# Row loads turned into columns on TensorE, and fifteen tiny loads behind the last weights, in a gated decode kernel

## The chip, the cores and the metric

One core of a Trainium2 chip runs the whole program. The time is device microseconds of one execution; the median of several runs is compared. One execution is also recorded by the hardware profiler, and all profile rows come from that one.

## What is computed

One token of width 512 goes through two branches that a gate mixes. Branch A is attention over a cache of 4096 positions with 32 heads of 128; branch B is a dense layer with squared ReLU. B_x is not used. The reference, cut down:

```python
x = A_x                                                  # [1, 1, 512], bf16
g = sigmoid((x * gate_w).sum(-1, keepdims=True))
q = (x @ wq).reshape(1, 1, 32, 128)                      # wq 512 x 4096
p = softmax(einsum("bhqd,bhkd->bhqk", q, k) * 128**-0.5) # k, v: 32 x 4096 x 128
a = einsum("bhqk,bhkd->bhqd", p, v) @ wo                 # wo 4096 x 512
h = relu(x @ w1 + b1); h = h * h                         # w1 512 x 1376
b = h @ w2 + b2                                          # w2 1376 x 512
out = g * a + (1 - g) * b
```

K and V are 32 MB each, wq and wo 4 MB each, w1 and w2 1.4 MB each. x, gate_w, b1 and b2 are 1 to 2.75 KB.

## The kernel before

**Queues.** SP issues nearly all loads, in an order written out by hand: the four slices of wq, seven heads of K, then for each head one load of V (`load_v`) and one of K seven heads ahead (`load_k`, LAG = 7), with w1 put behind head 8 and w2 behind head 10. A head's K or V is 1 MB, one load; 8 slots each. A K load waits until the head eight before it was used by DVE (s_sd) and by PE (s_t), a V load until the PV matmuls of the head eight before it are done (s_pv). The upper half of wo follows at the end: `wox` (L247), three chunks (L249) that each have a semaphore, and then the store of `out` (L252) when `fin4` is ready (s_f4). GpSimd (POOL) loads the lower half of wo into the place of wq once the last q rows are read. ACT issues only the five small loads at the start (L296 to L300): x, gate weights, b1 in two parts and b2. Three of the vectors are laid out as columns: `col` gives partition p the elements p·j of the flat vector, so that x is 128 pieces of 8 bytes, and the last 96 entries of b1 are 96 pieces of 2 bytes.

**Start.** DVE forms the gate's partial products (L536), PE sums them over partitions with a ones matrix (L345), ACT and DVE make the sigmoid `gcol` and `omg` = 1 − g. DVE spreads x over 128 columns (`xb`). PE makes q twice: as columns `qcol` (128 matmuls of 128x128 on one column of x, L351), copied out by DVE (L549), and as rows spread over all partitions (`q_rows`, L361, eight groups of four heads), copied to `qb` by ACT (L308).

**Heads.** For half of a head's positions, DVE multiplies K with the q rows and sums (`ttr`, L561, 16 per head). The other half is transposed on PE (`transposes`, L375), copied from PSUM by ACT (`evac`, L316) and multiplied with the q column on PE (`scores`, L385). DVE takes the copy of these scores and the maximum (`smax`). Every four heads PE and DVE find a common maximum (`max_rows`, `gmax`, `max_cols`) and ACT takes the exponentials. PV (`pv`, L412) runs LAG heads behind. One loop over i = 0 to 38 in each engine's program sets the order: head i is transposed and multiplied, head i − 1 scored, head i − 7 goes through PV.

**Branch B and the output.** At i = 24 PE multiplies w1 with the x columns (`mlp_h`, L428), DVE adds b1, takes ReLU and square (`mlp`), and PE multiplies w2 into the accumulator (`mlp_out`). The first 16 heads' outputs are turned and regrouped with a 0/1 selector `selA` (`turn_a`, `spread_a`, L452), then multiplied with the lower half of wo at i = 28 to 31 (`out_a`, L463). The other 16 heads go through `regroup` with the selector `selB` (built by GpSimd inside `w1_sb` once `mlp_h` has read it, L285), `out_b` (L488), the sum with the scaled b2 (L639), a transpose (L527), a copy (L641) and the store.

Of the kernel before, what the change touches and what calls it, by code (L numbers as in the profile page):

```python
# [5 lines left out]
def bass_gated_mix__gqa_block_cached__dense_activation_squared_relu__decode_kernel(  # L6
# [63 lines left out]
    with ctx:  # L70
# [18 lines left out]
        selB = w1_sb[0:NH - NA, 0, 0:1024].rearrange("h (c p) -> h c p", c=8)  # L89
        w2a = sb("w2a", [128, FG, DM], bf16)  # L90
# [3 lines left out]
        gwcol = sb("gwcol", [128, 4], bf16)  # L94
        b1a = sb("b1a", [128, FG], bf16)
        b1b = sb("b1b", [FR, 1], bf16)
        b2r = sb("b2r", [4, 128], bf16)
        selA = sb("selA", [NA, 4, 128], bf16)
# [12 lines left out]
        negs = sb("negs", [G, 128], fp32)  # L111
# [10 lines left out]
        gj = sb("gj", [128, 4], bf16)  # L122
        zp = sb("zp", [128, 1], fp32)
# [4 lines left out]
        hp = sb("hp", [128, FG + 1], fp32)  # L128
# [19 lines left out]
        Q = pX[:, 64:64 + NH]  # L148
# [32 lines left out]
        s_cst = sem("s_cst")  # L181
        s_xf = sem("s_xf")
# [30 lines left out]
        s_out = sem("s_out")  # L213

# [3 lines left out]
        @block.sync  # L218
        def _(eng):
            for t in range(4):  # L220
                eng.dma_start(wq_sb[:, t, :], wq_v[:, t, :]).then_inc(s_wq[t], 16)  # L221

            def load_k(h):
                if h >= NK:
                    eng.wait_ge(s_sd, h - NK + 1)
                    eng.wait_ge(s_t, 2 * (h - NK + 1))
                eng.dma_start(Kt[:, h % NK, :], k_h[h, :, :]).then_inc(s_k[h % NK], 16)  # L227

            def load_v(h):
                if h >= NV:  # L230
                    eng.wait_ge(s_pv, h - NV + 1)
                eng.dma_start(Vt[:, h % NV, :], v_h[h, :, :]).then_inc(s_v[h % NV], 16)  # L232

            for h in range(LAG):
                load_k(h)
            for h in range(NH):
                load_v(h)
                if h + LAG < NH:
                    load_k(h + LAG)
                if h == 8:  # L240
                    for t in range(4):
                        eng.dma_start(w1_sb[:, t, :], w1_v[:, t, :]).then_inc(s_w1, 16)
                if h == 10:
                    eng.dma_start(w2a[:, :, :], w2_v).then_inc(s_w2, 16)
                    eng.dma_start(w2b[:, :], B_w2[FG * 128:F, :]).then_inc(s_w2, 16)
            eng.wait_ge(s_wa, 1)
            eng.dma_start(wox, A_wo[HX * 128:HX * 128 + 128, :]).then_inc(s_wx, 16)  # L247
            for c in range(NW):
                eng.dma_start(wo_sb[:, TS[c]:TS[c + 1], :], wob_v[:, TS[c]:TS[c + 1], :])\  # L249
                   .then_inc(s_wo[c], 16)  # L250
            eng.wait_ge(s_f4, 1)
            eng.dma_start(out[0, 0, :].rearrange("(j p) -> j p", p=128), fin4[:, :]).then_inc(s_out, 16)  # L252
            eng.wait_ge(s_out, 16)

        @block.gpsimd
        def _(eng):
            eng.memset(ident[:, :], 0.0).then_inc(s_id, 1)
            eng.memset(identf[:, :], 0.0).then_inc(s_id, 1)
            eng.memset(onesf[:, :], 1.0).then_inc(s_cst, 1)  # L260
            eng.memset(negs[:, :], -SCALE).then_inc(s_cst, 1)
            eng.memset(selA[:, :, :], 0.0).then_inc(s_id, 1)
            eng.wait_ge(s_id, 3)
            for m in (ident, identf):
                eng.affine_select(out=m[:, :], in_=m[:, :], compare_op=ALU.not_equal, fill=1.0,
                                  base=0, pattern=[[-1, 128]], channel_multiplier=1)\
                   .then_inc(s_id, 1)
            eng.affine_select(out=selA[:, :, :], in_=selA[:, :, :], compare_op=ALU.not_equal, fill=1.0,
                              base=A0, pattern=[[1, 4], [-1, 128]], channel_multiplier=4)\
               .then_inc(s_id, 1)  # L270
            eng.wait_ge(s_qps, 8)
            HI = A0 + 4 * (HX + 1)
            LO = A0 + 4 * HX
            for r in range(4):
                eng.inc_swdge_sem([], [], mode="reset_dge_cursor")
                src = B_w1[0:4, 0:32].rearrange("p (a c) -> p a c", a=2)
                eng.dma_start(dm[0:4, r, :, 0:8], src[:, :, 0:8]).then_inc(s_dm[r], 16)  # L277
                eng.dma_start(W[HI + r:A0 + 64:4, :], woa_v[HI - A0 + r:64:4, :],
                              max_dma_last_dim=8192).then_inc(s_wp[2 * r], 16)
                eng.dma_start(W[A0 + r:LO:4, :], woa_v[r:LO - A0:4, :],  # L280
                              max_dma_last_dim=8192).then_inc(s_wp[2 * r + 1], 16)
            for q in s_dm:
                eng.wait_ge(q, 16)
            eng.wait_ge(s_h, 1)
            eng.memset(selB, 0.0).then_inc(s_sb, 1)  # L285
            eng.wait_ge(s_sb, 1)
            eng.affine_select(out=selB, in_=selB, compare_op=ALU.not_equal, fill=1.0,
                              base=0, pattern=[[1, 8], [-1, 128]], channel_multiplier=8)\
               .then_inc(s_sb, 1)
# [3 lines left out]
        def _(eng):  # L293
            def col(ap):
                return ap.rearrange("(p j) -> p j", p=128)
            eng.dma_start(xcol[:, :], col(A_x[0, 0, :])).then_inc(s_x, 16)  # L296
            eng.dma_start(gwcol[:, :], col(gate_w)).then_inc(s_x, 16)
            eng.dma_start(b1a[:, :], col(B_b1[0:FG * 128])).then_inc(s_b, 16)
            eng.dma_start(b1b[:, :], B_b1[FG * 128:F].rearrange("(p j) -> p j", j=1)).then_inc(s_b, 16)
            eng.dma_start(b2r[:, :], B_b2.rearrange("(j p) -> j p", p=128)).then_inc(s_b, 16)  # L300
            eng.wait_ge(s_x, 32)
            eng.activation(xcolf[:, :], xcol[:, :], ACT.Copy).then_inc(s_xf, 1)
# [39 lines left out]
        def _(eng):  # L342
            eng.wait_ge(s_cst, 2)
            eng.wait_ge(s_zp, 1)
            eng.matmul(Z, onesf[:, :], zp[:, :], start=True, stop=True).then_inc(s_z, 1)  # L345
            for t in range(4):
                eng.wait_ge(s_wq[t], 16)
            eng.wait_ge(s_ez, 1)
            for h in range(NH):
                for t in range(4):  # L350
                    mm = eng.matmul(Q[:, h:h + 1], wq_sb[:, t, h * 128:(h + 1) * 128],  # L351
                                    xcol[:, t:t + 1], start=(t == 0), stop=(t == 3))
            mm.then_inc(s_q, 1)
# [3 lines left out]
            def q_rows(c):  # L357
                if c >= 1:
                    eng.wait_ge(s_qb, c)
# [3 lines left out]
                mm.then_inc(s_qps, 1)  # L363

# [14 lines left out]
            def scores(h):  # L379
                if h >= 1:  # L380
                    eng.wait_ge(s_cp, h)
                for y in range(YB):
# [14 lines left out]
            def max_cols(g):  # L397
                eng.wait_ge(s_dg, g + 1)
                eng.matmul(MB[:, G * g:G * g + G], negs[:, :], dg[:, g, :],
                           start=True, stop=True).then_inc(s_mb, 1)  # L400

            def pv(h):
# [4 lines left out]
                if h == HPO:  # L407
                    eng.wait_ge(s_qc, 1)
                if h == 3 * HPO:
                    eng.wait_ge(s_qb, 8)  # L410
# [10 lines left out]
            def mlp_h():  # L421
                eng.wait_ge(s_w1, 64)
                eng.wait_ge(s_on, 2)
                for n in range(FG + 1):
                    M = 128 if n < FG else FR
                    for t in range(4):
                        lhs = w1_sb[:, t, n:FG * 128:FG] if n < FG else w1_sb[:, t, FG * 128:F]
                        mm = eng.matmul(H[0:M, n:n + 1], lhs, xcol[:, t:t + 1],  # L428
                                        start=(t == 0), stop=(t == 3))
# [19 lines left out]
            def spread_a():  # L449
                eng.wait_ge(s_ac, 1)  # L450
                for c in range(4):
# [17 lines left out]
            def regroup():  # L469
# [6 lines left out]
                eng.wait_ge(s_sb, 2)  # L476
# [18 lines left out]
            eng.wait_ge(s_id, 6)  # L495
            eng.wait_ge(s_b, 48)
            eng.transpose(KP[2][:, 0:4], b2r[:, :], ident[0:4, 0:4]).then_inc(s_b2, 1)
            eng.wait_ge(s_qc, 1)
            for i in range(NH + LAG):
# [4 lines left out]
                if i % 3 == 0 and i // 3 + 1 < 8:  # L504
                    q_rows(i // 3 + 1)
                if i >= 5 and (i - 5) % 4 == 0 and (i - 5) // 4 < NG:
# [24 lines left out]
        def _(eng):  # L531
# [4 lines left out]
            eng.tensor_tensor_reduce(gj[:, :], xcol[:, :], gwcol[:, :], 1.0, 0.0, ALU.mult,  # L536
# [11 lines left out]
            eng.wait_ge(s_q, 1)  # L548
            eng.tensor_copy(qcol[:, :], Q).then_inc(s_qc, 1)  # L549
# [22 lines left out]
            def gmax(g):  # L572
# [3 lines left out]
                eng.tensor_scalar(dg[:, g, :], identf[0:G, 0:G], gm[:, g:g + 1], None, ALU.mult)\  # L576
# [15 lines left out]
            def mlp():  # L592
                eng.wait_ge(s_h, 1)
                eng.tensor_tensor(hp[:, 0:FG], H[:, 0:FG], b1a[:, :], ALU.add).then_inc(s_hv, 1)
                eng.tensor_tensor(hp[0:FR, FG:FG + 1], H[0:FR, FG:FG + 1], b1b[:, :], ALU.add)\
                   .then_inc(s_hv, 1)
                eng.wait_ge(s_hv, 2)
                eng.tensor_scalar(hr[:, 0:FG], hp[:, 0:FG], 0.0, None, ALU.max).then_inc(s_hv, 1)
                eng.tensor_scalar(hr[0:FR, FG:FG + 1], hp[0:FR, FG:FG + 1], 0.0, None, ALU.max)\
                   .then_inc(s_hv, 1)  # L600
                eng.wait_ge(s_hv, 4)
# [7 lines left out]
            for i in range(NH + LAG):  # L609
                if i < NH:  # L610
                    ttr(i)
                if 1 <= i <= NH:
                    smax(i - 1)
                if i >= 5 and (i - 5) % 4 == 0 and (i - 5) // 4 < NG:
# [55 lines left out]
```

## Time and profile before

| | |
|---|---|
| median of 3 runs | 199.59 us (199.5 to 199.74) |
| the profiled execution | 199.66 us, its span 197.9 us |
| busy PE / PEld / DVE / ACT / POOL | 130.1 / 117.2 / 128.8 / 79.0 / 11.4 us |
| bytes moved, mean rate | 78.76 MB, 398 GB/s |
| DMA packets | 12560, of them 2336 under 512 B |
| K load, V load, from issue to landing (median) | 26.5 us, 27.3 us |
| wo chunks by SP, from issue to landing | 16.2, 17.6 and 17.8 us |
| the longest waits of PE and DVE | for K loads: 32.5 us (L375), 27.8 us (L561) |
| SP waits for fin before the store (L252) | 18.6 us |

The span runs from the first to the last recorded instruction; some 1.8 us of the execution lie outside it. PEld are weight loads, which overlap the matmuls (PE). "SPq" in the chain is the time that SP takes to issue a load, and a row "DMA" is the time from an issue to its landing, the stay in the queue included. Idle time of an engine that does not set the end costs nothing.

### The profile page before, as it was taken

The page shows a single profiled execution, that of the slowest core. Times are in us where ns is not written, and L with a number is a line of the kernel's source. Part 1 is how long each engine was busy: PE and PEld are TensorE (multiplying, and loading weights), DVE is VectorE, ACT ScalarE, POOL GpSimd, SP SyncE. Part 2 cuts the span into 40 slices and gives each one's busy share as a digit, 9 for nine tenths or more (in the row PEclk, how much of TensorE's full clock was granted, in tenths as well). Part 3 has the DMA queues.
Part 4 walks back from the last instruction along what each step waited for, and adds up shares of the span by engine and source line. Part 5 has one row for each costly group of instructions (what it writes and reads, how often), then busy time and mean ns, then how long its engine had stood idle before and what let it go on. Part 6 is the DMA issues. An engine that isn't in the chain of part 4 may idle for free.

```text
span 197.9 us, 6756 instructions
## 1 busy us (share of the span) xinstructions
PE 130.1 (66%) x2535; PEld 117.2 (59%) x2542; DVE 128.8 (65%) x1139; ACT 79.0 (40%) x147; POOL 11.4 (6%) x26
## 2 busy tenths in 40 slices
PE   0109946579897977716617476746978986995454
PEld 0107744459777767616615476746977886995443
DVE  0100899999999997707816778747799776760010
ACT  2000854737638536413307433533256331633000
POOL 4000000000000000000002910000210000000000
PEclk9999985855557555555557655555555555555555
DMA  6999999999999999999999999999999999999970
GB/s 194 413 375 427 421 421 419 424 417 421 421 414 416 421 417 411 419 418 397 406 422 412 419 416 411 413 422 416 424 411 422 419 416 419 421 419 419 411 307 33
DMA packets 12560, 78.76 MB, mean 398 GB/s; under 512 B 2336, under 2 KB 2560, under 8 KB 3328
## 3 DMA queue, kind: packets, MB, share of 16 engines
q1 hardware_dynamic: 11208, 76.36, 93.9%
q0 software_dynamic: 768, 1.97, 2.5%
q8 instruction: 20, 0.33, 0.7%
q10 hardware_dynamic: 552, 0.01, 0.2%
q14 instruction: 12, 0.10, 0.1%
HBM read 78.32 MB, written 0.00 MB: 396 GB/s over the span
## 4 chain that ended last, share of the span: by engine, by line
DMA 69%; DVE 14%; SPq 7%; PE 7%; issue 1%; ACT 0%; DVEq 0%
DMA Kt<-in_A_k_cache_dram 54%; DVE Kt L561 13%; DMA W<-in_A_wo_dram 9%; DMA W<-in_A_wq_dram 6%; SPq L232 5%; PE KP L375 2%; PE pX L351 2%; DVE S L561 1%; SPq L227 1%; PE pQ L361 1%; SPq L221 1%; PE pX L488 1%; PE pX L463 0%; PE pQ L412 0%; PE pX L412 0%
## 5 line engine op out<-in xcount | busy, mean ns | idle before, releaser
L561 DVE CUSTOM_DVE_ANT_0 Kt<-Kt,qb 128x128 bf16<-128x128 bf16 x512 | 112.1, 288 | 28.3 <-DMA Kt<-in_A_k_cache_dram 27.8
L316 ACT ACTIVATE kT<-KP 128x1024 bf16<-128x1024 bf16 x64 | 61.8, 1023 | 68.5 <-PE KP L375 68.5
L375 PE MATMUL KP<-ident,Kt 128*128 128x128 bf16 x512 | 55.6, 294 | 32.8 <-DMA Kt<-in_A_k_cache_dram 32.5
L375 PEld LDWEIGHTS KP<-ident,Kt 128*128 128x128 bf16 x512 | 48.2, 137 | 35.5 <-DMA Kt<-in_A_k_cache_dram 34.2
L561 DVE DVE_READ_ACCUMULATOR2_ANT S<- 128x1 f32 x512 | 41.6, 81 | 0.0
L385 PEld LDWEIGHTS pS<-qcol,kT 128*128 128x128 bf16 x512 | 18.6, 107 | 11.1 <-DVE S L567 10.8
L385 PE MATMUL pS<-qcol,kT 128*128 128x1 bf16 x512 | 19.1, 167 | 9.2 <-DVE S L567 8.9
L412 PEld LDWEIGHTS pO<-E,Vt 128*128 128x128 bf16 x512 | 15.5, 104 | 1.2 <-issue 0.8
L412 PE MATMUL pO<-E,Vt 128*128 128x1 bf16 x512 | 16.1, 165 | 0.0
L361 PE MATMUL pQ<-W,xb 128*128 128x512 bf16 x25 | 11.2, 581 | 1.7 <-issue 1.7
L412 PE MATMUL pQ<-E,Vt 128*128 128x1 bf16 x256 | 8.0, 165 | 6.3 <-DMA Vt<-in_A_v_cache_dram 6.3
L412 PEld LDWEIGHTS pQ<-E,Vt 128*128 128x128 bf16 x256 | 7.6, 104 | 6.7 <-issue 6.6
L308 ACT ACTIVATE qb<-pQ 128x512 bf16<-128x512 f32 x8 | 4.7, 592 | 16.4 <-PE pQ L361 16.4
L327 ACT ACTIVATE E<-S,nM 128x32 bf16<-128x32 f32 x32 | 9.9, 309 | 0.3
L277 POOL DMA_DIRECT2D dm<-in_B_w_dram x4 | 2.6, 648 | 104.4 <-PE pQ L361 104.4
L412 PEld LDWEIGHTS pX<-E,Vt 128*128 128x128 bf16 x256 | 7.8, 104 | 0.7 <-issue 0.6
L412 PE MATMUL pX<-E,Vt 128*128 128x1 bf16 x256 | 8.1, 165 | 0.0
L351 PE MATMUL pX<-xcol,W 128*128 128x1 bf16 x128 | 3.6, 165 | 4.9 <-DMA W<-in_A_wq_dram 4.9
L345 PE MATMUL pX<-zp,onesf 128*128 128x1 f32 x2 | 0.6, 347 | 9.3 <-DVE zp L536 9.3
L570 DVE TENSOR_REDUCE mp<-S 128x1 f32<-128x32 f32 x32 | 6.0, 186 | 1.1
L351 PEld LDWEIGHTS pX<-xcol,W 128*128 128x128 bf16 x128 | 3.5, 104 | 4.9 <-issue 4.9
L582 DVE RECIPROCAL rden<-pM 128x8 f32<-128x8 f32 x4 | 0.8, 200 | 8.1 <-PE pM L418 8.1
(83 smaller groups left out, 76.2 us busy)
## 6 DMA issues: line engine op xcount, KB each, us to landing
Kt<-in_A_k_cache_dram SPq DMA_DIRECT2D x32, 1024.0 KB, 26.5
Vt<-in_A_v_cache_dram SPq DMA_DIRECT2D x32, 1024.0 KB, 27.3
W<-in_A_wq_dram SPq DMA_DIRECT2D x4, 1024.0 KB, 8.4
W<-in_A_wo_dram POOLq DMA_DIRECT2D x4, 384.0 KB, 12.8
w_sb<-in_B_w_dram SPq DMA_DIRECT2D x4, 344.0 KB, 22.2
w2a<-in_B_w_dram SPq DMA_DIRECT2D x1, 1280.0 KB, 18.7
W<-in_A_wo_dram SPq DMA_DIRECT2D x1, 1024.0 KB, 16.2
W<-in_A_wo_dram SPq DMA_DIRECT2D x1, 768.0 KB, 17.6
```

The source lines that it names most:

```text
L232: eng.dma_start(Vt[:, h % NV, :], v_h[h, :, :]).then_inc(s_v[h % NV], 16)
L277: eng.dma_start(dm[0:4, r, :, 0:8], src[:, :, 0:8]).then_inc(s_dm[r], 16)
L308: eng.activation(qb[:, c * 512:(c + 1) * 512], pQ[:, :], ACT.Copy).then_inc(s_qb, 1)
L316: eng.activation(kT[:, h % 2, j * HB * 128:(j + 1) * HB * 128], KP[n % 3][:, :], ACT.Copy).then_inc(s_ev, 1)
L327: eng.activation(E[:, h % NE, :], S[:, h % NS, :], ACT.Exp, bias=nM[:, h:h + 1], scale=SCALE, accum_out=RS[:, h:h + 1]).then_inc(s_e, 1)
L351: mm = eng.matmul(Q[:, h:h + 1], wq_sb[:, t, h * 128:(h + 1) * 128], xcol[:, t:t + 1], start=(t == 0), stop=(t == 3))
L361: mm = eng.matmul(pQ[:, :], xb[:, t, :], wq_sb[:, t, c * 512:(c + 1) * 512], start=(t == 0), stop=(t == 3))
L375: mm = eng.transpose(KP[n % 3][:, y * 128:(y + 1) * 128], Kt[:, h % NK, b * 128:(b + 1) * 128], ident[:, :])
L385: mm = eng.matmul(S2[:, y:y + 1], kT[:, h % 2, y * 128:(y + 1) * 128], qcol[:, h:h + 1], start=True, stop=True)
L412: mm = eng.matmul(O(h, h + 1), Vt[:, h % NV, b * 128:(b + 1) * 128], E[:, h % NE, b:b + 1], start=(b == 0), stop=(b == NB - 1))
L561: ins = eng.tensor_tensor_reduce(kb, kb, qb[:, h * 128:(h + 1) * 128], 1.0, 0.0, ALU.mult, ALU.add, S[:, h % NS, b:b + 1])
L570: eng.tensor_reduce(mp[:, h:h + 1], S[:, h % NS, :], AX.X, ALU.max).then_inc(s_mp, 1)
```

## The change

- **Rows for columns.** x, gate_w and b1 are loaded as one row each, on one partition (x and the gate into a corner of `w1_sb`, which w1 overwrites later), b2 as before but into `w1_sb`. PE makes the x columns from the row with four matmuls against a 1x1 identity (XC); ACT copies them out twice (fp32, bf16). The gate's sum is one DVE reduction over the row. b1 enters `mlp_h` as one more matmul per group of outputs, and DVE's two adds go.
- **q columns from q rows.** The 128 matmuls of L351 go. `q_cols(c)` takes the four heads' columns out of `qb` with four matmuls against an identity column, and DVE copies them (`qcol_copy`), in eight groups: group 0 ahead of the loop, the others two rounds behind their q rows. `q_rows(c)` now waits for that copy (s_qc) in place of s_qb, `scores(h)` waits for its group's copy.
- **Memory and constants.** `selA` is built inside `w1_sb` at the place where `selB` is, ahead of it, and `spread_a` waits for it; the constant `negs` goes, its factor sits in DVE's `gmax`. SP waits for s_z and s_b2 ahead of the w1 loads.
- **Fifteen tiny loads.** Behind the last wo chunk SP issues loads of n rows of 16 bytes, n = 1 to 15, into a part of `w1_sb` that nothing reads, and waits for them after the store.

The diff, cut to its core:

```diff
+        selA = w1_sb[0:NA, 1, 0:512].rearrange("h (c p) -> h c p", c=4)
+        xrow = w1_sb[0:1, 0, 0:DM]
+        grow = w1_sb[0:1, 1, 0:DM]
+        b1r = sb("b1r", [1, F], bf16)
+        b2r = w1_sb[0:4, 2, 0:128]
+        XC = pO[:, 0:4]
+        Q = pQ[:, 0:4]
...
 @block.sync
                 if h == 8:
+                    eng.wait_ge(s_z, 1)
+                    eng.wait_ge(s_b2, 1)
...
+            for n in range(1, 16):
+                eng.dma_start(w1_sb[0:n, 3, 32 * n:32 * n + 8], B_w1[0:n, 0:8]).then_inc(s_pr[n - 1], 16)
             eng.wait_ge(s_f4, 1)
             eng.dma_start(out[0, 0, :].rearrange("(j p) -> j p", p=128), fin4[:, :]).then_inc(s_out, 16)
             eng.wait_ge(s_out, 16)
+            for q in s_pr:
+                eng.wait_ge(q, 16)
...
 @block.gpsimd
-            eng.memset(selB, 0.0).then_inc(s_sb, 1)
+            eng.memset(w1_sb[0:NA, 0:2, 0:1024], 0.0).then_inc(s_sb, 1)
             eng.wait_ge(s_sb, 1)
+            eng.affine_select(out=selA, in_=selA, compare_op=ALU.not_equal, fill=1.0,
+                              base=A0, pattern=[[1, 4], [-1, 128]], channel_multiplier=4)\
+               .then_inc(s_sb, 1)
...
 @block.scalar
-            eng.dma_start(xcol[:, :], col(A_x[0, 0, :])).then_inc(s_x, 16)
-            eng.dma_start(gwcol[:, :], col(gate_w)).then_inc(s_x, 16)
-            eng.dma_start(b1a[:, :], col(B_b1[0:FG * 128])).then_inc(s_b, 16)
-            eng.dma_start(b1b[:, :], B_b1[FG * 128:F].rearrange("(p j) -> p j", j=1)).then_inc(s_b, 16)
-            eng.dma_start(b2r[:, :], B_b2.rearrange("(j p) -> j p", p=128)).then_inc(s_b, 16)
-            eng.wait_ge(s_x, 32)
-            eng.activation(xcolf[:, :], xcol[:, :], ACT.Copy).then_inc(s_xf, 1)
+            eng.dma_start(xrow, A_x[0, :, :]).then_inc(s_x, 16)
+            eng.dma_start(grow, gate_w.rearrange("(a n) -> a n", a=1)).then_inc(s_x, 16)
+            eng.dma_start(b1r[:, :], B_b1.rearrange("(a n) -> a n", a=1)).then_inc(s_b, 16)
+            eng.dma_start(b2r, B_b2.rearrange("(j p) -> j p", p=128)).then_inc(s_b, 16)
+            eng.wait_ge(s_xc, 1)
+            eng.activation(xcolf[:, :], XC, ACT.Copy).then_inc(s_xf, 1)
+            eng.wait_ge(s_xf, 1)
+            eng.activation(xcol[:, :], xcolf[:, :], ACT.Copy).then_inc(s_xf, 1)
...
 @block.tensor
+            for t in range(4):
+                mm = eng.matmul(XC[:, t:t + 1], xrow[:, t:DM:4], ident[0:1, 0:1], start=True, stop=True)
+            mm.then_inc(s_xc, 1)
...
-            for h in range(NH):
-                for t in range(4):
-                    mm = eng.matmul(Q[:, h:h + 1], wq_sb[:, t, h * 128:(h + 1) * 128],
-                                    xcol[:, t:t + 1], start=(t == 0), stop=(t == 3))
-            mm.then_inc(s_q, 1)
...
+            def q_cols(c):
+                eng.wait_ge(s_qb, c + 1)
+                for n in range(4):
+                    h = 4 * c + n
+                    mm = eng.matmul(Q[:, n:n + 1], qb[:, h * 128:(h + 1) * 128], ident[:, 0:1],
+                                    start=True, stop=True)
+                mm.then_inc(s_q, 1)
...
+                    eng.matmul(H[0:M, n:n + 1], b1r[:, n:FG * 128:FG] if n < FG else b1r[:, FG * 128:F],
+                               ident[0:1, 0:1], start=True, stop=False)
...
+                if i % 3 == 2 and i // 3 + 1 < 8:
+                    q_cols(i // 3 + 1)
...
 @block.vector
-            eng.tensor_tensor_reduce(gj[:, :], xcol[:, :], gwcol[:, :], 1.0, 0.0, ALU.mult,
+            eng.tensor_tensor_reduce(grow, xrow, grow, 1.0, 0.0, ALU.mult,
...
-                eng.tensor_tensor(hp[:, 0:FG], H[:, 0:FG], b1a[:, :], ALU.add).then_inc(s_hv, 1)
-                eng.tensor_tensor(hp[0:FR, FG:FG + 1], H[0:FR, FG:FG + 1], b1b[:, :], ALU.add)\
```

More of the change, by code (lines that the diff above doesn't have):

```diff
@@ L93, in bass_gated_mix__gqa_block_cached__dense_activation_squared_relu__decode_kernel @@
         xcolf = sb("xcolf", [128, 4], fp32)
[L94 to L98, printed above, removed]
+        xrow = w1_sb[0:1, 0, 0:DM]
+        grow = w1_sb[0:1, 1, 0:DM]
+        b1r = sb("b1r", [1, F], bf16)
+        b2r = w1_sb[0:4, 2, 0:128]
         onA = sb("onA", [128, NA], bf16)
@@ L110, in bass_gated_mix__gqa_block_cached__dense_activation_squared_relu__decode_kernel @@
         onesf = sb("onesf", [128, 128], fp32)
-        negs = sb("negs", [G, 128], fp32)
         qcol = sb("qcol", [128, NH], bf16)
@@ L121, in bass_gated_mix__gqa_block_cached__dense_activation_squared_relu__decode_kernel @@
         onorm = sb("onorm", [128, NH], bf16)
-        gj = sb("gj", [128, 4], bf16)
-        zp = sb("zp", [128, 1], fp32)
+        zp = sb("zp", [1, 1], fp32)
         ez = sb("ez", [128, 1], fp32)
@@ L127, in bass_gated_mix__gqa_block_cached__dense_activation_squared_relu__decode_kernel @@
         omg = sb("omg", [128, 1], fp32)
-        hp = sb("hp", [128, FG + 1], fp32)
         hr = sb("hr", [128, FG + 1], fp32)
@@ L147, in bass_gated_mix__gqa_block_cached__dense_activation_squared_relu__decode_kernel @@
         Z = pX[:, 0:1]
-        Q = pX[:, 64:64 + NH]
+        XC = pO[:, 0:4]
+        Q = pQ[:, 0:4]
         H = pX[:, 128:128 + FG + 1]
@@ L181, in bass_gated_mix__gqa_block_cached__dense_activation_squared_relu__decode_kernel @@
         s_cst = sem("s_cst")
+        s_xc = sem("s_xc")
         s_xf = sem("s_xf")
@@ L213, in bass_gated_mix__gqa_block_cached__dense_activation_squared_relu__decode_kernel @@
         s_out = sem("s_out")
+        s_pr = [sem(f"s_pr{n}") for n in range(15)]
         block = ctx.enter_context(nc.Block())
@@ L260, in _ @@
             eng.memset(onesf[:, :], 1.0).then_inc(s_cst, 1)
-            eng.memset(negs[:, :], -SCALE).then_inc(s_cst, 1)
-            eng.memset(selA[:, :, :], 0.0).then_inc(s_id, 1)
-            eng.wait_ge(s_id, 3)
+            eng.wait_ge(s_id, 2)
             for m in (ident, identf):
@@ L267, in _ @@
                    .then_inc(s_id, 1)
-            eng.affine_select(out=selA[:, :, :], in_=selA[:, :, :], compare_op=ALU.not_equal, fill=1.0,
-                              base=A0, pattern=[[1, 4], [-1, 128]], channel_multiplier=4)\
-               .then_inc(s_id, 1)
             eng.wait_ge(s_qps, 8)
@@ L293, in _ @@
         def _(eng):
-            def col(ap):
-                return ap.rearrange("(p j) -> p j", p=128)
-            eng.dma_start(xcol[:, :], col(A_x[0, 0, :])).then_inc(s_x, 16)
-            eng.dma_start(gwcol[:, :], col(gate_w)).then_inc(s_x, 16)
-            eng.dma_start(b1a[:, :], col(B_b1[0:FG * 128])).then_inc(s_b, 16)
-            eng.dma_start(b1b[:, :], B_b1[FG * 128:F].rearrange("(p j) -> p j", j=1)).then_inc(s_b, 16)
-            eng.dma_start(b2r[:, :], B_b2.rearrange("(j p) -> j p", p=128)).then_inc(s_b, 16)
-            eng.wait_ge(s_x, 32)
-            eng.activation(xcolf[:, :], xcol[:, :], ACT.Copy).then_inc(s_xf, 1)
+            eng.dma_start(xrow, A_x[0, :, :]).then_inc(s_x, 16)
[6 more added lines that the diff above has]
+            eng.activation(xcol[:, :], xcolf[:, :], ACT.Copy).then_inc(s_xf, 1)
             eng.wait_ge(s_z, 1)
@@ L342, in _ @@
         def _(eng):
-            eng.wait_ge(s_cst, 2)
+            eng.wait_ge(s_cst, 1)
+            eng.wait_ge(s_id, 3)
+            eng.wait_ge(s_x, 32)
+            for t in range(4):
+                mm = eng.matmul(XC[:, t:t + 1], xrow[:, t:DM:4], ident[0:1, 0:1], start=True, stop=True)
+            mm.then_inc(s_xc, 1)
             eng.wait_ge(s_zp, 1)
-            eng.matmul(Z, onesf[:, :], zp[:, :], start=True, stop=True).then_inc(s_z, 1)
+            eng.matmul(Z, onesf[0:1, :], zp[:, :], start=True, stop=True).then_inc(s_z, 1)
             for t in range(4):
                 eng.wait_ge(s_wq[t], 16)
-            eng.wait_ge(s_ez, 1)
-            for h in range(NH):
-                for t in range(4):
-                    mm = eng.matmul(Q[:, h:h + 1], wq_sb[:, t, h * 128:(h + 1) * 128],
-                                    xcol[:, t:t + 1], start=(t == 0), stop=(t == 3))
-            mm.then_inc(s_q, 1)
             eng.wait_ge(s_xb, 4)
@@ L358, in q_rows @@
                 if c >= 1:
-                    eng.wait_ge(s_qb, c)
+                    eng.wait_ge(s_qc, c)
                 for t in range(4):
@@ L381, in scores @@
                     eng.wait_ge(s_cp, h)
+                eng.wait_ge(s_qc, h // 4 + 1)
                 for y in range(YB):
@@ L398, in max_cols @@
                 eng.wait_ge(s_dg, g + 1)
-                eng.matmul(MB[:, G * g:G * g + G], negs[:, :], dg[:, g, :],
+                eng.matmul(MB[:, G * g:G * g + G], onesf[0:G, :], dg[:, g, :],
                            start=True, stop=True).then_inc(s_mb, 1)
@@ L406, in pv @@
                     eng.wait_ge(s_on, h // HPO - 1)
-                if h == HPO:
-                    eng.wait_ge(s_qc, 1)
                 if h == 3 * HPO:
-                    eng.wait_ge(s_qb, 8)
+                    eng.wait_ge(s_qc, 8)
                 for b in range(NB):
@@ L428, in mlp_h @@
                         mm = eng.matmul(H[0:M, n:n + 1], lhs, xcol[:, t:t + 1],
-                                        start=(t == 0), stop=(t == 3))
+                                        start=False, stop=(t == 3))
                 mm.then_inc(s_h, 1)
@@ L450, in spread_a @@
                 eng.wait_ge(s_ac, 1)
+                eng.wait_ge(s_sb, 2)
                 for c in range(4):
@@ L475, in regroup @@
                                start=False, stop=False, skip_group_check=True)
-                eng.wait_ge(s_sb, 2)
+                eng.wait_ge(s_sb, 3)
                 eng.wait_ge(s_oc, 1)
@@ L494, in _ @@
             q_rows(0)
[L495 to L498, printed above, removed]
+            q_cols(0)
+            eng.wait_ge(s_id, 4)
+            eng.wait_ge(s_b, 32)
+            eng.transpose(KP[2][:, 0:4], b2r, ident[0:4, 0:4]).then_inc(s_b2, 1)
             for i in range(NH + LAG):
@@ L547, in _, with qcol_copy @@
             eng.tensor_scalar(omg[:, :], gcol[:, :], -1.0, 1.0, ALU.mult, ALU.add).then_inc(s_g, 1)
-            eng.wait_ge(s_q, 1)
-            eng.tensor_copy(qcol[:, :], Q).then_inc(s_qc, 1)
+            def qcol_copy(c):
+                eng.wait_ge(s_q, c + 1)
+                eng.tensor_copy(qcol[:, 4 * c:4 * c + 4], Q).then_inc(s_qc, 1)
+            qcol_copy(0)
             eng.wait_ge(s_g, 3)
@@ L575, in gmax @@
                 eng.wait_ge(s_gm, g + 1)
-                eng.tensor_scalar(dg[:, g, :], identf[0:G, 0:G], gm[:, g:g + 1], None, ALU.mult)\
+                eng.tensor_scalar(dg[:, g, :], identf[0:G, 0:G], gm[:, g:g + 1], -SCALE, ALU.mult, ALU.mult)\
                    .then_inc(s_dg, 1)
@@ L593, in mlp @@
                 eng.wait_ge(s_h, 1)
-                eng.tensor_tensor(hp[:, 0:FG], H[:, 0:FG], b1a[:, :], ALU.add).then_inc(s_hv, 1)
-                eng.tensor_tensor(hp[0:FR, FG:FG + 1], H[0:FR, FG:FG + 1], b1b[:, :], ALU.add)\
+                eng.tensor_scalar(hr[:, 0:FG], H[:, 0:FG], 0.0, None, ALU.max).then_inc(s_hv, 1)
+                eng.tensor_scalar(hr[0:FR, FG:FG + 1], H[0:FR, FG:FG + 1], 0.0, None, ALU.max)\
                    .then_inc(s_hv, 1)
                 eng.wait_ge(s_hv, 2)
[L598 to L601, printed above, removed]
                 eng.scalar_tensor_tensor(out=hs[:, 0:FG], in0=hr[:, 0:FG], scalar=omg[:, 0:1],
@@ L613, in _ @@
                     smax(i - 1)
+                if i % 3 == 2 and i // 3 + 1 < 8:
+                    qcol_copy(i // 3 + 1)
                 if i >= 5 and (i - 5) % 4 == 0 and (i - 5) // 4 < NG:
```

## The prediction

> **What bounds the kernel now.** I read the page first, then the chain of waits in order of time, the windows of the first and the last microseconds, the timeline of SP and the DMA packet records. Part 2 of the page, in 40 slices of 4.95 us:
>
> ```profile
> DMA  6999999999999999999999999999999999999970
> GB/s 194 413 375 427 421 421 419 424 417 421 421 414 416 421 417 411 419 418 397 406 422 412 419 416 411 413 422 416 424 411 422 419 416 419 421 419 419 411 307 33
> ```
>
> The 16 DMA engines are busy from the second slice to the 38th at about 420 GB/s, so 1 MB takes 2.5 us. No compute engine comes near that: PE is busy 66%, DVE 65%. Part 3 says whose bytes these are:
>
> ```profile
> q1 hardware_dynamic: 11208, 76.36, 93.9%
> q0 software_dynamic: 768, 1.97, 2.5%
> q8 instruction: 20, 0.33, 0.7%
> q10 hardware_dynamic: 552, 0.01, 0.2%
> q14 instruction: 12, 0.10, 0.1%
> ```
>
> q1 is SP's queue (all of K, V and the weights), q10 is ACT's, which carries only the five small loads that the change rewrites. The shares add to 97.4%; the rest is the 1.8 us before the first packet and the end. The end of the chain:
>
> ```profile
> 171.88 0.04 issue
> 171.93 1.89 PE KP L375 x16
> 173.81 0.41 PE pS L385 x16
> 174.22 0.85 PE pQ L412 x32
> 175.07 0.87 PE pX L463 x32
> ...
> 175.96 0.33 SPq L247
> 176.28 0.04 issue
> 176.33 0.43 SPq L249
> 176.76 0.04 issue
> 176.80 17.64 DMA W<-in_A_wo_dram
> 194.44 0.05 issue
> 194.48 1.02 PE pX L488 x32
> ```
>
> The wo chunk is issued at 176.80 and lands 17.64 us later: seven loads' worth of queue stands before it. K loads wait 26.5 us (median, part 6), eleven loads' worth. So whatever PE, DVE or ACT does some microseconds sooner or later changes only how long a load stands in the queue. The end is set by the time the queue needs, plus a fixed tail (last wo matmuls, fin, transpose, copy, out store) of 3.4 us. Windows of the last stretch (length, busy time of PE, PEld, DVE, ACT, POOL, clock, DMA share, GB/s):
>
> ```profile
> 190.00:191.00 1.00, 0.91 (x32) 0.82 (x31) 0.00 (x0) 0.00 (x0) 0.00 (x0) 0.50 0.65 270
> 192.00:193.00 1.00, 0.68 (x15) 0.49 (x16) 0.17 (x1) 0.00 (x0) 0.00 (x0) 0.50 0.52 209
> 194.00:195.00 1.00, 0.52 (x19) 0.52 (x20) 0.00 (x0) 0.00 (x0) 0.00 (x0) 0.50 0.09 33
> ```
>
> From 190 to 195 the DMA share falls step by step: some engines are done at 190, the slowest at 195. What counts is the work of the slowest engine.
>
> **The change, part by part.** All sums are made against the profiled execution: 199.66 us, a span of 197.9 and 1.76 outside it. The median of the runs is 199.59, 0.07 less.
>
> *Column loads become row loads.* Before, x, gate and b1 arrive in pieces of 8, 8, 20 and 2 bytes per partition: 128 + 128 + 128 + 96 pieces, with b2's 4 that is 484; four loads with 16 completion marks and one with 4 make 68 more, together the 552 packets of q10. After, three rows and b2: 52 pieces and 52 marks if a row is spread over 16 engines, 14 packets if not. At least 448 of 552 go. q10's 0.2% of 197.9 us is 0.40 us on every engine (0.30 to 0.49 by the rounding), and 448/552 of it is 0.32 us (0.24 to 0.40). If a row is not spread, one engine takes 4.8 KB more, which at 26 KB/us (420 GB/s over 16) is 0.18 us, still less than it sheds. I take 0.30, all of it on the path, as every engine carries some 34 of these packets between its big ones.
>
> *The hole in the stream.* These windows show the rate while and after q10 is at work:
>
> ```profile
> 11.00:12.00 1.00, 0.00 (x0) 0.00 (x0) 0.00 (x0) 0.00 (x0) 0.00 (x0) 1.00 1.04 410
> 12.00:13.00 1.00, 0.00 (x0) 0.00 (x0) 0.00 (x0) 0.00 (x0) 0.00 (x0) 1.00 0.82 262
> 13.00:14.00 1.00, 0.00 (x0) 0.00 (x0) 0.00 (x0) 0.00 (x0) 0.00 (x0) 1.00 0.91 370
> 14.00:15.00 1.00, 0.27 (x11) 0.30 (x12) 0.00 (x0) 0.00 (x0) 0.00 (x0) 1.00 1.01 426
> 15.00:16.00 1.00, 1.00 (x44) 1.00 (x41) 0.00 (x0) 0.00 (x0) 0.00 (x0) 1.00 1.03 434
> ```
>
> Against 430 GB/s the stretch from 11 to 14 loses (20 + 168 + 60)/430 = 0.58 us, with engines idle between packets although SP has loads waiting to be accepted. The packet records put the 96 two-byte pieces of b1b (with their marks) between 10.5 and 13.7 us, and the engines never idle like this again before 189. I lay the hole to these pieces, though the first of them pass at full rate, so it may be the turn from wq to K. Bounds 0 and 0.58; taken 0.45, since part of the 0.58 is already in the 0.30.
>
> The Trainium skill (DMA: Bandwidth & Descriptors, Specifications) says that below 512 B the engine does read-modify-write; 8-byte pieces pass here at 414 GB/s (6 to 8 us), so the trace shows no large price of that for them. The same page (Rules for kernel authors) says that a one-partition row fans out over 16 engines in few descriptors, and that it isn't measured which shape is faster.
>
> *q columns from q rows.* 128 matmuls (L351, 14.73 to 18.28, 3.55 us) go; the first DVE product comes about 3 us sooner: q_rows(0) 1.5, qb copy 0.6, 4 small matmuls 0.2, copy 0.2. Eight q_cols of 4 matmuls (16 of L385 take 0.57, so 0.15 each) and eight DVE copies (L549, 0.19) come in, 1.2 and 1.5 us over 20 heads. PE waits 32.5 us and DVE 27.8 us for K loads; the cover is these waits. Worth: 0. New waits: q_rows(c) for the copy of the q columns, behind which a head's scores queue, and scores(h) for its columns, made two heads earlier. Both are in the same cover; without it each could cost 0.2 us a group.
>
> *b1 on PE, x columns, selectors.* 11 bias matmuls (44 of L428 take 2.8 us, so 0.7) and two DVE adds less, inside the wait for K at 139 to 142. The x columns are ready long before wq lands at 14.49 (now xcol is used at 8.86). POOL's selectors start at 142.14: memset twice 0.94, selA 0.62, ready at about 144.8; spread_a (L452) runs at 155.4. SP's two new waits at h == 8 are long met. All 0; selA would cost from 10 us of delay on.
>
> *Fifteen tiny loads.* 120 pieces of 16 bytes and 120 marks behind wo on SP's queue. Issue: SP stands idle from 177.7 to 196.29, waiting for fin. The nearest rows are an issue of 0.32 us (out, 4 rows) and 0.33 to 0.45 (wo chunks); 15 of these end at 184.4 at the latest. The other end is an issue into a full queue, 2.1 us: 32 us, out 14 us late. I take the short one, because wox and wo, issued into the same queue, took 0.33 to 0.43. In the DMA engines they come after all of wo; at q10's 0.011 us a packet (0.40 × 16 / 552) 30 packets are 0.33 us, over before 196.3. Here a rule speaks against the change: the skill's page on DMA gives about 2.0 us fixed for each transfer (Anatomy of one DMA), and calls those under 64 KB mostly overhead (Rules for kernel authors); as an estimate from that page, fifteen in a row would add 30 us. Against adding them up stands the row of ACT's issues: five loads issued within 2.8 us are in flight together.
>
> *Fifteen waits at the end.* A second wait before a K issue costs SP about 0.045 us (0.09 between issues instead of 0.045), so 15 are 0.7 us. The chain shows that the wait written second (L226) runs by itself before the issue that holds the first; so the fifteen run before the wait for out, inside its 0.8 us (SP's wait for out_dram). Taken 0, bound 0.7.
>
> Sum: −0.30 − 0.45 = −0.75; 199.66 − 0.75 = 198.91, some 198.85 against the median. Forecast 198.9. A difference under 0.2% (0.4 us) can't be told from no change here.
>
> **Rivals.**
> 1. *The hole isn't b1b's.* Then only 0.24 to 0.40 us comes: 199.2 to 199.4, no change to be measured. For it: the rate holds for the first half of the two-byte pieces.
> 2. *The end is not moved at all.* The slowest engine owes its lag to instruction fetches (q8, q14) and the saving sits on others, or a new row takes back what was saved: 199.5 to 199.7.
> 3. *Slower: SP is late with the tiny loads.* If the queue counts loads, not bytes, and takes ten or eleven (26.5/2.5 stand in it in the middle), nine are in it at 177.7, the next enter one by one as V and wo land, and four or five are left when the last wo chunk lands at 195.07 (its last mark in the trace). At 0.4 us each, out goes at 197.0 instead of 196.29: +0.7, and with the end waits no longer covered up to +1.4. With 0 to 0.3 of the DMA saving: 200.0 to 201.0. It decides from three loads left at 195 on. Against it: no issue after 159 took over 0.43 us.
>
> **How the numbers follow.** Forecast 0.50, rival 1 0.20, rival 2 0.12, rival 3 0.18. Faster: 0.50 and a little of rival 1, 0.52. Same: 0.30. Slower: 0.18. The range goes down to 198.5 (0.40 + 0.58 and 0.1 of ramp) and up to 199.9, which leaves most of rival 3 out. The forecast's own range is 198.5 to 199.2.
>
> **What would show it.** Right: q10 at some 100 packets and 0.0%; no window under 400 GB/s between 10 and 14 us; wo landing about 0.7 us sooner after its place in the queue; SP's tiny issues over by 185; the first L561 at 17 to 18 us with no effect. Wrong: the same hole at 12 us (rival 1), wo landing at 194.4 to 195 as before (rival 2), an issue of a tiny load after 195 or out issued over 1.3 us behind the last wo landing (rival 3).

## The result and the profile after

The median went from 199.67 us (six runs) to 198.68 us (six runs); the ratio is 0.9954, with a 95% interval of 0.9941 to 0.9967. That is 0.92 us by the ratio (below, a ratio's difference is always taken times 199.6 us). A ratio's interval is some 0.1% to either side, 0.2 to 0.3 us, so the difference between two changed kernels is known to 0.3 to 0.4 us. The forecast was 198.9, a gain of 0.75. The profiled execution took 198.97, its span 197.1.

Part 2 of the page after, 40 slices of 4.93 us, and two rows of part 3:

```profile
DMA  6999999999999999999999999999999999999970
GB/s 221 427 427 424 421 421 422 412 421 421 416 417 421 416 422 403 420 424 385 414 421 416 419 416 411 408 426 417 421 417 417 421 412 419 417 421 421 412 296 21
```

```profile
q8 instruction: 19, 0.31, 0.6%
...
q10 hardware_dynamic: 14, 0.01, 0.0%
```

The first three slices, 194, 413 and 375 GB/s before, are now 221, 427 and 427; from the fourth on nothing differs but noise. q10 has 14 packets instead of 552: a one-partition row is not spread, it is one packet and one mark. Where the time came from shows in three windows of each kernel. Before:

```profile
2.00:6.00 4.00, 0.00 (x0) 0.00 (x0) 0.00 (x0) 1.28 (x1) 1.13 (x3) 1.00 0.91 318
6.00:10.00 4.00, 0.56 (x2) 0.50 (x2) 0.85 (x6) 0.31 (x2) 0.00 (x0) 1.00 1.03 423
10.00:14.00 4.00, 0.00 (x0) 0.00 (x0) 0.47 (x3) 0.07 (x1) 0.00 (x0) 1.00 0.93 357
```

After:

```profile
2.00:6.00 4.00, 0.26 (x4) 0.20 (x4) 0.35 (x1) 1.36 (x2) 0.00 (x0) 1.00 0.92 366
6.00:10.00 4.00, 0.58 (x2) 0.49 (x2) 1.46 (x9) 0.48 (x3) 0.00 (x0) 1.00 1.01 426
10.00:14.00 4.00, 0.77 (x2) 0.29 (x3) 0.00 (x0) 0.00 (x0) 0.00 (x0) 1.00 1.02 430
```

The last two columns are the DMA share and GB/s. From 2 to 6 us the rate rises by 48 GB/s (4 × 48 = 192 KB, 0.46 us at 420), from 10 to 14 by 73 (292 KB, 0.70 us). The stream is some 1.1 us ahead when wq has landed, and it stays so: summed from the packet records, the 6th MB has passed at 17.87 us before and at 16.76 after, the 78th at 192.27 and 191.22. The end of the chain keeps 0.8 us of it:

```profile
175.53 18.10 DMA W<-in_A_wo_dram
193.63 0.05 issue
193.68 1.03 PE pX L500 x32
```

The chunk lands at 193.63 instead of 194.44; issued 1.27 us sooner, it stands 0.46 us longer in the queue. The other 0.3 us may be no more than scatter between executions: the profiled one is the slowest of its six, 0.29 us above their median, and in the profile of `rows_only` below, which took 198.67, the chunk lands at 193.24, 1.2 us sooner than before. SP's timeline behind wo:

```profile
175.06 2.49 SPq L251 DMA_DIRECT2D W<-in_A_wo_dram  x3
177.59 5.26 SPq L254 DMA_DIRECT2D w_sb<-in_B_w_dram  x15
195.49 0.27 SPq L256 DMA_DIRECT2D out_dram<-fin  x1
```

Fifteen issues take 5.26 us and end at 182.85, and out is issued 0.80 us sooner than at 196.29 before.

### The profile page after: what moved, and what is told of

Its sections match the earlier page's. It is cut to its first block, busy times and chain, and to the rows that moved or that the text cites. A ratio compares the mean times of both kernels' runs of the same rounds, so it can differ in the third digit from the quotient of the medians.

```text
span 197.1 us, 6623 instructions
## 1 busy us (share of the span) xinstructions
PE 132.0 (67%) x2455; PEld 119.0 (60%) x2461; DVE 129.2 (66%) x1144; ACT 79.5 (40%) x148; POOL 11.7 (6%) x24
## 4 chain that ended last, share of the span: by engine, by line
DMA 70%; DVE 12%; SPq 9%; PE 6%; issue 1%; ACT 0%
DMA Kt<-in_A_k_cache_dram 55%; DVE Kt L579 11%; DMA W<-in_A_wo_dram 9%; SPq L232 6%; DMA W<-in_A_wq_dram 6%; PE KP L385 2%; SPq L227 2%; PE pQ L363 1%; DVE S L579 1%; SPq L221 1%; PE pX L500 1%; PE pX L475 0%; PE pQ L421 0%; PE pX L421 0%; PE pS L396 0%
## 5 line engine op out<-in xcount | busy, mean ns | idle before, releaser
L385 PE MATMUL KP<-ident,Kt 128*128 128x128 bf16 x512 | 56.6, 299 | 31.7 <-DMA Kt<-in_A_k_cache_dram 31.7
L385 PEld LDWEIGHTS KP<-ident,Kt 128*128 128x128 bf16 x512 | 49.1, 139 | 34.5 <-DMA Kt<-in_A_k_cache_dram 33.1
L363 PE MATMUL pQ<-W,xb 128*128 128x512 bf16 x26 | 12.3, 614 | 7.7 <-DMA W<-in_A_wq_dram 6.3
L363 PEld LDWEIGHTS pQ<-W,xb 128*128 128x128 bf16 x32 | 3.6, 130 | 10.7 <-issue 10.7
L585 DVE COPY S<-pS 128x16 f32<-128x16 f32 x32 | 5.4, 169 | 2.7 <-PE pS L396 2.7
L565 DVE CAST qcol<-pQ 128x4 bf16<-128x4 f32 x8 | 1.2, 152 | 8.4 <-PE pQ L371 8.4
```

The costliest lines, as they stand in the source:

```text
L363: mm = eng.matmul(pQ[:, :], xb[:, t, :], wq_sb[:, t, c * 512:(c + 1) * 512], start=(t == 0), stop=(t == 3))
L385: mm = eng.transpose(KP[n % 3][:, y * 128:(y + 1) * 128], Kt[:, h % NK, b * 128:(b + 1) * 128], ident[:, :])
L585: eng.tensor_copy(S[:, h % NS, XB:NB], S2).then_inc(s_cp, 1)
```

## The experiments

The theory: the gain is DMA time in the first 14 us (fewer small packets, no hole); the q columns and the tiny loads are covered. Its rivals: the sooner products bring it, or the tiny loads change the tail.

The diffs are cut to their core.

**Which part of the change.** Four kernels, each with one part alone or left out.

`rows_only`, from the kernel after:

```diff
-        Q = pQ[:, 0:4]
+        Q = pX[:, 64:64 + NH]
-            for n in range(1, 16):
-                eng.dma_start(w1_sb[0:n, 3, 32 * n:32 * n + 8], ...)
+            for h in range(NH):          # the 128 matmuls on wq, as before
...
-            def q_cols(c): ...
```

> The kernel after without the fifteen tiny loads and with the 128 matmuls of wq for the q columns put back: of the change, the row loads, the bias matmuls and the selector in w1_sb remain. Theory (the gain is DMA time at the start: fewer small packets and no hole at 12 us): 198.6 to 198.9, as the whole change, with no window under 400 GB/s between 10 and 14 us. Rival (the q columns from q rows bring it, because the first products come 4 us sooner): 199.5 to 199.7.

Measured 198.68, ratio 0.9958 (0.9946 to 0.9971): the whole gain. Its page has these two rows:

```profile
q8 instruction: 20, 0.33, 0.7%
...
q10 hardware_dynamic: 14, 0.01, 0.0%
```

With 20 instruction packets, as before, it is as fast as the kernel after with 19, so the one fetch less isn't the gain either.

`no_probes`, from the kernel after:

```diff
-            for n in range(1, 16):
-                eng.dma_start(w1_sb[0:n, 3, 32 * n:32 * n + 8], B_w1[0:n, 0:8]).then_inc(s_pr[n - 1], 16)
-            for q in s_pr:
-                eng.wait_ge(q, 16)
```

> The kernel after without the fifteen tiny loads and their waits. Theory (they are covered at issue, in the engines and in the last waits): 198.6 to 198.8, the same as the whole change within 0.15. Rival (they delay the out store or the last wo packets): faster by 0.2 to 0.5, 198.2 to 198.5. Rival (packets behind the last wo loads help them land): slower, 198.9 or more.

Measured 198.68, ratio 0.9952 (0.9938 to 0.9965): no difference.

`qcols_only`, from the kernel before:

```diff
-            for h in range(NH):          # the 128 matmuls on wq
+            def q_cols(c): ...
+            def qcol_copy(c): ...
+                eng.wait_ge(s_qc, h // 4 + 1)
```

> The kernel before with the q columns from q rows alone. Theory (PE and DVE are covered by the queue): 199.5 to 199.8, with the first product of DVE 3 to 4 us sooner and the last wo chunk landing as before. Rival (the sooner products bring it): 198.7 to 199.2.

Measured 199.61, ratio 1.0000 (0.9992 to 1.0009). The first product of DVE comes 3.4 us sooner (17.43 instead of 20.79), and that is worth nothing in a kernel that waits for its queue.

`probes_only`, from the kernel before:

```diff
+            for n in range(1, 16):
+                eng.dma_start(w1_sb[0:n, 3, 32 * n:32 * n + 8], B_w1[0:n, 0:8]).then_inc(s_pr[n - 1], 16)
+            for q in s_pr:
+                eng.wait_ge(q, 16)
```

> The kernel before with the fifteen tiny loads and their waits alone. Theory: 199.5 to 199.8, the last tiny load landing 1.5 to 2 us behind the last wo chunk and still ahead of the out store. Rival (they delay the end): 199.9 to 200.4. Rival (they help it): 199.2 or less.

Measured 199.56, ratio 0.9998 (0.9989 to 1.0006): no difference. The last tiny load lands at 197.02, 0.4 us ahead of out (197.41).

**How near the tiny loads are to costing something.** `probes30`, from the kernel after:

```diff
+            for r in range(2):
                 for n in range(1, 16):
-                eng.dma_start(w1_sb[0:n, 3, 32 * n:32 * n + 8], ...)
+                    eng.dma_start(w1_sb[0:n, 3, 512 * r + 32 * n:512 * r + 32 * n + 8], ...)
```

> The kernel after with each of the fifteen tiny loads issued twice. After, the last of them lands 0.6 us ahead of the out store and they land 0.18 us apart. Theory (their cover is nearly used up): fifteen more at 0.18 end 2.7 us later, at about 198.8 in the span, and out, behind them in the same rings, lands with them: 200.6 to 201.2. Rival (they are free at any number, as they were not seen in the time): 198.6 to 198.8.

Measured 200.74, ratio 1.0061 (1.0048 to 1.0075), 2.1 us above the kernel after. SP's timeline:

```profile
176.57 11.40 SPq L255 DMA_DIRECT2D w_sb<-in_B_w_dram  x30
195.22 0.27 SPq L258 DMA_DIRECT2D out_dram<-fin  x1
```

The issues are over at 188, and out is issued even sooner than after, so the time is lost behind the issue: fifteen more loads at the 0.18 us by which they land apart are 2.7, less the 0.6 that was left. The marks in the trace show where: three of out's four have come by 196.34, the fourth comes at 198.61, just behind the last mark of the tiny loads at 198.42.

**Which column loads cost what.** `no_b1b`, from the kernel before:

```diff
-            eng.dma_start(b1b[:, :], B_b1[FG * 128:F].rearrange("(p j) -> p j", j=1)).then_inc(s_b, 16)
+            eng.memset(b1b[:, :], 0.0).then_inc(s_dz, 1)
```

> The kernel before without the load of the 96 two-byte pieces (the last 96 entries of b1 are left out, zeros stand in their place); the other column loads stay. Theory (the hole at 12 us is made by these pieces, and each of the other small packets costs its 9 ns): 0.06 for 112 packets and 0.4 to 0.58 for the hole: 198.9 to 199.1, no window under 400 GB/s between 10 and 14 us. Rival (the gain is the count of small packets alone): 199.4 to 199.5. Rival (the hole belongs to the turn from wq to K): the hole stays, 199.4 to 199.5.

Measured 199.23, ratio 0.9983 (0.9974 to 0.9992), 0.34 us, by the interval 0.16 to 0.52: more than the packets alone. The time lies above the theory's 198.9 to 199.1, a miss, though the interval just reaches the lower end of the gain it gave (0.46). The windows:

```profile
5.00:6.00 1.00, 0.00 (x0) 0.00 (x0) 0.00 (x0) 0.00 (x0) 0.00 (x0) 1.00 0.98 378
6.00:7.00 1.00, 0.00 (x0) 0.01 (x1) 0.30 (x4) 0.21 (x1) 0.00 (x0) 1.00 0.95 378
7.00:8.00 1.00, 0.56 (x2) 0.49 (x2) 0.72 (x5) 0.17 (x1) 0.00 (x0) 1.00 1.00 403
...
12.00:13.00 1.00, 0.00 (x0) 0.00 (x0) 0.00 (x0) 0.00 (x0) 0.00 (x0) 1.00 0.99 418
```

The hole at 12 us is gone, so it wasn't the turn from wq to K. From 5 to 7, where pieces of 8 and 20 bytes pass, the rate is 378, where before had 377 and 410 and the kernel after has 421 and 451. Over the stretch from 1 to 6 us it is 281, hardly above the 274 of before, against 308 after. So the other column loads cost rate as well.

`ex_2b` and `ex_8b`, from the kernel after, behind the load of b2:

```diff
+            for n in range(4):           # ex_2b
+                eng.dma_start(ex[:, n:n + 1], B_b1[FG * 128:F].rearrange("(p j) -> p j", j=1)).then_inc(s_ex, 16)
```

```diff
+            for n in range(4):           # ex_8b
+                eng.dma_start(ex[:, 4 * n:4 * n + 4], A_x[0, 0, :].rearrange("(p j) -> p j", p=128)).then_inc(s_ex, 16)
```

> The kernel after with four more loads of 96 two-byte pieces each into a tile that nothing reads, issued by ACT behind b2. Theory (the two-byte pieces make the hole): four holes of 0.4 to 0.58 and 448 packets of 9 ns over 16 engines (0.25): 200.5 to 201.2. Rival (packets alone count): 198.9 to 199.0.

Measured 200.35, ratio 1.0046 (1.0031 to 1.0061): 1.84 us for four loads, 0.46 each.

> The kernel after with four more loads of 128 eight-byte pieces each into a tile that nothing reads, issued by ACT behind b2. Theory (pieces of eight bytes cost their packets alone): 576 packets of 9 ns over 16 engines, 0.32: 198.9 to 199.1. Rival (pieces under 512 bytes cost as the two-byte pieces do): 200.5 or more.

Measured 199.97, ratio 1.0025 (1.0016 to 1.0033): 1.42 us, 0.35 each. This was a miss: the theory gave 0.08 each. Eight-byte pieces make holes too. Windows of `ex_8b`:

```profile
8.00:10.00 2.00, 0.00 (x0) 0.00 (x0) 0.00 (x0) 0.00 (x0) 0.00 (x0) 1.00 0.96 344
10.00:12.00 2.00, 0.00 (x0) 0.00 (x0) 0.00 (x0) 0.00 (x0) 0.00 (x0) 1.00 0.92 324
```

**What makes the holes.** The price may go with the number of pieces, their size, the place they are read from, the place they are written to, or the moment. Four kernels vary `ex_8b` in one of these each, as far as that can be done alone. (All `ex_` kernels also end ACT's program with a wait for the added loads. In `ex_one_part` and `ex_512b` the loads write into a V slot that is still empty, and SP waits for them ahead of V's head 7, which it issues at 41 us, long after they have landed.)

`ex_8b_far`, another place to read from:

```diff
-                eng.dma_start(ex[:, 4 * n:4 * n + 4], A_x[0, 0, :].rearrange("(p j) -> p j", p=128)).then_inc(s_ex, 16)
+                eng.dma_start(ex[:, 4 * n:4 * n + 4], B_w1[128 * n:128 * n + 128, 0:4]).then_inc(s_ex, 16)
```

> The kernel after with four loads of 128 eight-byte pieces at the start, each piece from another row of w1 (2752 bytes apart) and not from the 1 KB of x. Theory A (the number of pieces counts): 199.8 to 200.1, as with x. Theory C (16 engines read neighbouring bytes at once and wait for each other): 198.8 to 199.3.

Measured 199.16, ratio 0.9975 (0.9966 to 0.9983): 0.42 us, and no hole. (The tensor is another one too, and these loads read no byte twice, where `ex_8b` reads the same 1 KB four times.)

```profile
8.00:10.00 2.00, 0.00 (x0) 0.00 (x0) 0.00 (x0) 0.00 (x0) 0.00 (x0) 1.00 1.00 410
10.00:12.00 2.00, 0.00 (x0) 0.00 (x0) 0.00 (x0) 0.00 (x0) 0.00 (x0) 1.00 1.06 435
```

`ex_8b_late`, another moment:

```diff
                     evac(i)
+                    if i == 12:
+                        for n in range(4):
+                            eng.dma_start(ex[:, 4 * n:4 * n + 4], A_x[0, 0, :]...).then_inc(s_ex, 16)
```

> The kernel after with the same four loads of 128 eight-byte pieces, issued by ACT behind its copies of head 12 (about 60 us) and not at the start, where they cost 1.29 us (0.32 a load, 36 ns a piece of one engine, against 9 ns in its packet row). Theory A (such a piece costs 36 ns beside big packets wherever it is): 199.8 to 200.1. Theory B (it is the first microseconds of the stream, with cold reads and SP and ACT both issuing, that make it dear): 198.7 to 199.1.

Measured 199.09, ratio 0.9972 (0.9961 to 0.9983): 0.36 us. The loads were issued from 64.7 us on, and their pieces pass from 68 to 78 us. There the rate is 382 to 414 GB/s in windows of 2 us, 384 to 426 in the kernel after: no hole like those of `ex_8b`.

`ex_one_part`, another place to write to:

```diff
-                eng.dma_start(ex[:, 4 * n:4 * n + 4], A_x[0, 0, :].rearrange("(p j) -> p j", p=128)).then_inc(s_ex, 16)
+                eng.dma_start(ex[0:1, 1024 * n:1024 * n + 1024].rearrange("a (p j) -> a p j", j=8)[:, :, 0:4],
+                              A_x[0, :, :].rearrange("a (p j) -> a p j", j=4)).then_inc(s_ex, 16)
```

> The kernel after with four loads of x in 128 eight-byte pieces at the start, all of them written to one partition, at a distance of 16 bytes. Theory A (the number of pieces counts): 199.8 to 200.1. Theory D (the writes of few bytes to 128 partitions, beside the big packets to the same partitions, make the cost): 198.7 to 199.2.

Measured 200.27, ratio 1.0038 (1.0023 to 1.0053): 1.68 us, with 312 GB/s from 8 to 10 us, so the 128 partitions written to aren't the cause.

`ex_512b`, another size (and, with it, other places to read from and write to):

```diff
-                eng.dma_start(ex[:, 4 * n:4 * n + 4], A_x[0, 0, :].rearrange("(p j) -> p j", p=128)).then_inc(s_ex, 16)
+                eng.dma_start(ex[:, 256 * n:256 * n + 256], B_w2[128 * n:128 * n + 128, 0:256]).then_inc(s_ex, 16)
```

> The kernel after with four loads of 128 pieces of 512 bytes (from w2, into a V slot that is still empty; SP waits for them ahead of the load of V's head 7). Their bytes alone are 262 KB, 0.62 us at 420 GB/s. Theory A (a piece costs some 27 ns above its packet row, whatever its size): 0.62 + 0.08 + 1.0, 200.2 to 200.5. Theory E (only pieces under 512 bytes are dear): 0.62 + 0.08, 199.3 to 199.5.

Measured 199.70, ratio 1.0004 (0.9996 to 1.0013): 1.00 us, above the 0.70 of Theory E and below the 1.70 of Theory A. The row of q10 in its page, which has the packets of `ex_8b` in number, fits it:

```profile
q10 hardware_dynamic: 590, 0.27, 0.5%
```

0.5% of 198 us is 0.99 us on every engine, close to the measured price; no hole shows in its windows (419 and 422 GB/s from 8 to 12). For `ex_8b_far` the row says 0.2%, 0.40 us, and 0.42 was measured. For `ex_8b` and `ex_one_part` it says 0.2% as well, and 1.42 and 1.68 were measured.

So in the stream a small packet costs about what its row shows, and above that come the holes. Two things decide about them, the place that the pieces are read from and the moment: as many pieces from far rows make none, and the same pieces at 68 to 78 us make none. That they come because 16 engines read neighbouring bytes at once is a reading that fits, and isn't shown, as `ex_8b_far` changes the tensor and the repeated reading too. Repetition can't be all of it, since b1b is read once and has its hole at 12 us. Why the moment matters stays open. In `ex_8b_late` the 16 marks of a load come within 0.5 us at 13 us and within 4.2 us at 74 us, so the engines run in step at the start and not later, which would fit, but no run here tested it.

## Why the prediction was right, point by point

- **The bound.** Right. The queue sets the end: the 1.1 us won by 14 us are still there at 191 us, and 3.4 us sooner on PE and DVE at the start are worth 0 (`qcols_only` 1.0000). ACT and POOL were not tried apart.
- **Small packets, −0.30.** Right as far as it can be seen. q10's 0.40 us went to nothing (14 packets, the case of rows that are not spread), and in `ex_8b_far` and `ex_512b` the price agrees with the share in the row to 0.1 us, closer than the intervals tell. Apart from the holes it was not measured.
- **The hole, −0.45, laid to b1b.** Right that b1b makes the hole at 12 us: without b1b it is gone. The gain was 0.34 us, where 0.45 + 0.06 was thought; its interval, up to 0.52, doesn't exclude that. Wrong that the other column loads cost their packets alone: 0.58 us more came when they went too (`no_b1b` against after), and the row of q10 in `no_b1b`, 0.1%, gives 0.20 for them. The argument from "8-byte pieces pass here at 414 GB/s" failed. It looked at 6 to 8 us alone, while such pieces pass from 2.4 us on, at 318 GB/s from 2 to 6 us where the kernel after has 366, and four such loads made holes in `ex_8b`.
- **What the sum left out.** It has no term for the low rate from 2 to 6 us. 0.46 us of it went with the column loads (366 GB/s after, 372 in `rows_only`), some of it packet time that is in the 0.30. With it the start gives 1.1 us. The gain measured by the ratio, 0.92, has an interval of 0.66 to 1.18, which holds both that and the 0.75. That the sum came so near is in part luck: it counts what b1b costs beyond its packets, and nothing of that kind for the other column loads.
- **q columns.** Right in its price. The first product of DVE comes 4.4 us sooner (16.43 instead of 20.79), not 3, since wq also lands sooner.
- **b1 on PE and the selectors.** They are part of `rows_only`, which has the whole gain; alone they were not run. The wait for K at 139 to 142, named as their cover, isn't in PE's timeline before: PE works without a gap from 136.19 to 143.7 there. What covers them is the queue.
- **Tiny loads, issue.** Right: 5.26 us in all, where fifteen times 0.32 to 0.45 make 4.8 to 6.7. Rival 3, SP late by the count of loads, fell: in `probes30` the queue took thirty at 0.38 us each.
- **Tiny loads in the engines, 0.33 us.** Too small. On the last engine they land 0.18 us apart, and the last one at 196.06 (its last mark in the trace), 1.8 us behind the last wo mark at 194.27 and only 0.6 before out. Nothing was lost here, but the cover was nearly used up, as `probes30` shows with +2.1.
- **Fifteen waits.** Right. They ran ahead of the wait for out, from 195.81 to 196.27, and SP's wait there fell from 0.8 to 0.4 us (the waits' row L70). They cost nothing.
- **The rule against the change.** The Trainium skill (DMA: Bandwidth & Descriptors, Anatomy of one DMA) gives about 2.0 us fixed for a transfer, fitted there on loads that GpSimd issues. The fifteen, which SP issues, do not add it up: they land 0.18 us apart. The same page (Specifications) says that below 512 B the engine does read-modify-write. `ex_8b_far` has pieces far below that, and its 512 pieces and their 64 marks over 16 engines cost 0.42 us, about the time of their packets, so in the stream it shows no further price for the small write.

## What to carry to other kernels

In a kernel that is bound by its load queue, look at the first slices of the rate: small loads at the start may cost several times their share in the queue's row, and the rest stands as a low rate of the big loads beside them. Load a vector as a row and turn it on TensorE where TensorE waits anyway; or let the small pieces come later. Whatever is put behind the last load is free only up to the store that follows in the same queue, so measure the room that is left there by doubling it.

## What the runs showed of the hardware that was not expected

Column loads of one small vector at the start of a stream cost 0.35 us (128 pieces of 8 bytes) to 0.46 us (96 of 2 bytes) each, known to some 0.1 us. As many 8-byte pieces from far rows, or the same ones 60 us later, cost 0.09 to 0.11. Fifteen loads of 1 to 15 rows of 16 bytes land 0.18 us apart behind one another, far more than the packet rows of 9 ns let one think.
